# A lightning-attention and mixture-of-depths kernel: from a scheduled order to one pipeline written out by hand over all chunks

## The chip, the cores and the metric

The kernel runs on one core of one Trainium2 chip. The metric is device time in microseconds (us), the median of several executions. The engines are TensorE (PE, with PEld for its weight loads), VectorE (DVE), ScalarE (ACT), GpSimd (POOL) and SyncE (SP, which issues DMAs).

## The reference, cut to what matters

Attention over q, k, v of shape (4 batches, 8 heads, 768 tokens, 64), with a decay `lam` per head, and then a mixture of depths: the 128 tokens of each batch with the highest score go through a two-layer expert, whose result, times a gate, is added to their rows.

```python
# attention, blockwise: scores inside a block, a running state across blocks
intra = (q_b @ k_b.T * lam**(i - j)) @ v_b          # i >= j
inter = (q_b * lam**(i + 1)) @ state
state = lam**block * state + (k_b * lam**(block - 1 - j)).T @ v_b
x = out.transpose(0, 2, 1, 3).reshape(4, 768, 512)  # heads side by side
# mixture of depths, each batch
scores = x @ w_gate
top = 128 tokens with the highest scores
out = x.copy()
out[top] = x[top] + sigmoid(scores[top])[:, None] * (relu(x[top] @ w1) @ w2)
```

All data are fp32; w1 is 512 x 1024 and w2 is 1024 x 512.

## The kernel before, in words

The tokens are cut into chunks of 128, so a batch has six chunks and the whole input 24. `attention_chunk` does one chunk for all eight heads, with two heads (a pair) on the 128 partitions. It loads q, k and v (`qn`, `kn`, `vn`, 256 KB each, SP queue), transposes q and k on PE into `tp` (copied by ACT to `qT`, `kT`), multiplies them to the scores `ss`, masks these on DVE into `p`, and sums `po` from `p` and `vn` and, but for the first chunk of a batch, from `qs` (q times the decay, POOL) and the state. ACT copies `po` to `x_b`, POOL issues its store to `out`, and DVE sums it with `w_gate` to the score column `sc` (tile `xg`). For all but the last chunk of a batch the state is renewed: `kd` (POOL), matmuls `pu`, state times decay (POOL), and the sum of both (DVE).

After the six chunks of a batch come `rank_tokens` and `expert`. The ranks: PE transposes the scores into rows (`pb`, copied to `sc_row`), and DVE counts for each of the six columns of tokens how many scores are larger (`cmp`, L234 to L242). The expert builds two one-hot matrices on DVE: `pick_g` (with the gate `g`, fp32) and `pick`. 24 matmuls `pg` multiply `x_b` by `pick_g`, which gathers the 128 rows, transposed, onto the slots (L271). Six matmuls `pe` give the token of each slot (`tok`). Then come the hidden layer `ph` (w1) with `hs`, the second layer `py` (w2), the copy `y`, and an indirect DMA on POOL that adds `y` to the rows of `out` in HBM (L314).

The kernel is written as plain loops over batches and chunks. The order of the instructions on each engine is set by a planner that goes by dependencies, priorities and free buffers. Both weight matrices are loaded at the beginning, in one DMA of 2 MB each, on ACT's queue, beside the first loads of q, k and v. The buffers: `ld` has 4 of each load, the PSUM pools are two `tp`, two `ss`, one `pu`, one `po` and two shared ones (`pm`) for the expert.

Of the kernel before, what the change touches and what calls it, by code (L numbers as in the profile page):

```python
# [8 lines left out]
FP32 = mybir.dt.float32  # L9
# [8 lines left out]
def kernel(  # L18
# [12 lines left out]
    nc = tc.nc  # L31
# [10 lines left out]
    NGR = (CAP + 127) // 128   # groups of 128 slots  # L42
# [12 lines left out]
    ps_m = ctx.enter_context(tc.tile_pool(name="ps_m", bufs=2, space=PSUM))  # L55

# [22 lines left out]
    # kpow[j, h] = lam_h ** (L - 1 - j)  # L79
# [3 lines left out]
    # with the two heads of a pair on the partitions:  # L83
    # qpow[p, hp, i] = lam ** (i + 1), decay[p, hp, :] = lam ** L
# [13 lines left out]
    # below[i, j] = 1 for j < i  # L98
    below = const.tile([128, 128], FP32, name="below")
    nc.vector.memset(below[:], 1.0)  # L100
    nc.gpsimd.affine_select(
        out=below[:], in_=below[:], compare_op=ALU.is_gt, fill=0.0,
        base=0, pattern=[[-1, 128]], channel_multiplier=1,
    )
    # the slots of each group; in slots_in those past the capacity match no rank
    slots_i = const.tile([128, S], I32, name="slots_i")
    nc.gpsimd.iota(slots_i[:], pattern=[[1, S]], base=0, channel_multiplier=0)
    slots = const.tile([128, S], FP32, name="slots")
    nc.vector.tensor_copy(slots[:], slots_i[:])
    slots_in = const.tile([128, S], FP32, name="slots_in")  # L110
    nc.vector.tensor_copy(slots_in[:], slots_i[:])
    nc.vector.memset(slots_in[:, CAP:], -1.0)
    # the token's place in two columns: start of its chunk, place in the chunk
    place_i = const.tile([128, 1], I32, name="place_i")
    nc.gpsimd.iota(place_i[:], pattern=[[0, 1]], base=0, channel_multiplier=1)
    place = const.tile([128, NT, 2], BF16, name="place")
    for t in range(NT):
        nc.vector.memset(place[:, t, 0:1], float(t * L))
        nc.vector.tensor_copy(place[:, t, 1:2], place_i[:])

# [1 line left out]
    def attention_chunk(b, c, state, x_b, sc):  # L122
        rows = slice(c * L, (c + 1) * L)
        last = c == NT - 1
        qn = ld.tile([128, H, D], FP32, name="qn")
        kn = ld.tile([128, H, D], FP32, name="kn")
        vn = ld.tile([128, H, D], FP32, name="vn")
        for t, src in ((qn, q), (kn, k), (vn, v)):
            nc.sync.dma_start(out=t[:], in_=src[b, :, rows, :].rearrange("h p d -> p h d"))  # L129

        qT = att.tile([128, NHP, L], FP32, name="qT")
        kT = att.tile([128, NHP, L], FP32, name="kT")
        for t, dst in ((qn, qT), (kn, kT)):
            tp = ps_t.tile([128, NHP, L], FP32, name="tp")
            for hp in range(NHP):
                nc.tensor.transpose(  # L136
                    tp[:, hp, :], in_=t[:, 2 * hp : 2 * hp + 2, :], identity=ident[:]
                )
            nc.scalar.copy(out=dst[:], in_=tp[:])  # L139

        if c > 0:
            qs = att.tile([128, NHP, L], FP32, name="qs")
            nc.gpsimd.tensor_tensor(out=qs[:], in0=qT[:], in1=qpow[:], op=ALU.mult)  # L143

        # scores with the keys on the partitions, even and odd heads in two banks
        ss = [ps_s.tile([128, NHP, L], FP32, name="ss") for _ in range(2)]
# [27 lines left out]
        nc.gpsimd.dma_start(out=out[b, rows, :], in_=x_b[:, c, :])  # L174
# [5 lines left out]
        if last:  # L180
            return None

        # state of each pair: the two heads' blocks on the diagonal, zeros beside them
        kd = att.tile([128, H, D], FP32, name="kd")
        nc.gpsimd.tensor_tensor(  # L185
            out=kd[:], in0=kn[:], in1=kpow[:].unsqueeze(2).broadcast_to([128, H, D]),
            op=ALU.mult,
        )
        pu = ps_u.tile([128, NHP, 128], FP32, name="pu")
        for hp in range(NHP):  # L190
            nc.tensor.matmul(  # L191
                pu[:, hp, :],
                lhsT=kd[:, 2 * hp : 2 * hp + 2, :],
                rhs=vn[:, 2 * hp : 2 * hp + 2, :].rearrange("p h e -> p (h e)"),
                start=True, stop=True,
            )
        new = att.tile([128, NHP, 128], FP32, name="state", bufs=3)
        if c == 0:
            nc.gpsimd.memset(new[:], 0.0)
        else:  # L200
            nc.gpsimd.tensor_tensor(out=new[:], in0=state[:], in1=decay[:], op=ALU.mult)  # L201
        for hh in range(2):
            r = slice(hh * 64, (hh + 1) * 64)
            if c == 0:
                nc.vector.tensor_copy(new[r, :, r], pu[r, :, r])
            else:
                nc.vector.tensor_tensor(
                    out=new[r, :, r], in0=pu[r, :, r], in1=new[r, :, r], op=ALU.add
                )
        return new  # L210

# [1 line left out]
    def rank_tokens(sc):  # L213
        sc_row = mod.tile([128, S], FP32, name="sc_row")
        half = (NT + 1) // 2
        for t0 in range(0, NT, half):
            n = min(half, NT - t0)
            pb = ps_m.tile([128, n, 128], FP32, name="pb", tag="pm")
            for t in range(n):
                nc.tensor.transpose(  # L220
                    pb[:, t, :], in_=sc[:, t0 + t : t0 + t + 1].broadcast_to([128, 128]),
                    identity=ident[:],
                )
            nc.scalar.copy(
                out=sc_row[:, t0 * L : (t0 + n) * L], in_=pb[:].rearrange("p t j -> p (t j)")
            )

        parts = mod.tile([128, 3, NT], FP32, name="parts")
        nc.vector.memset(parts[:, 0, 0:1], 0.0)  # L229
        cmp = mod.tile([128, S], FP32, name="cmp")  # L230
        for t in range(NT):
            s = sc[:, t : t + 1]
            if t > 0:
                nc.vector.tensor_scalar(  # L234
                    out=cmp[:, : t * L], in0=sc_row[:, : t * L], scalar1=s, scalar2=None,
                    op0=ALU.is_ge, op1=ALU.add, accum_out=parts[:, 0, t : t + 1],
                )
            nc.vector.tensor_scalar(  # L238
                out=cmp[:, t * L :], in0=sc_row[:, t * L :], scalar1=s, scalar2=None,
                op0=ALU.is_gt, op1=ALU.add, accum_out=parts[:, 1, t : t + 1],  # L240
            )
            nc.vector.scalar_tensor_tensor(  # L242
                out=cmp[:, t * L : (t + 1) * L], in0=sc_row[:, t * L : (t + 1) * L],
# [76 lines left out]
    for b in range(B):  # L320
# [3 lines left out]
        for c in range(NT):  # L324
            state = attention_chunk(b, c, state, x_b, sc)
# [42 lines left out]
```

## Time and profile before

| | |
|---|---|
| median of 3 runs | 316.76 us (316.01 to 317.12) |
| span of the profiled execution | 315.3 us |
| time around that span | not recorded; the median lies 1.5 us above it |
| PE busy | 254.1 us (81%) |
| PE weight loads busy | 220.3 us (70%) |
| DVE, ACT, POOL busy | 124.3, 55.3, 90.3 us |
| HBM read and written | 23.33 and 7.34 MB |

Busy shares are means over stages that have different limits. Matmuls are pipelined and their ends modelled, so a busy PE may still run slowly; the granted clock of PE (1.00 for 2.4 GHz, 0.50 for 1.2 GHz) has to be read beside it.

### The profile page before, as it was taken

The page shows a single profiled execution, that of the slowest core. Times are in us where ns is not written, and L with a number is a line of the kernel's source. Part 1 is how long each engine was busy: PE and PEld are TensorE (multiplying, and loading weights), DVE is VectorE, ACT ScalarE, POOL GpSimd, SP SyncE. Part 2 cuts the span into 40 slices and gives each one's busy share as a digit, 9 for nine tenths or more (in the row PEclk, how much of TensorE's full clock was granted, in tenths as well). Part 3 has the DMA queues.
Part 4 walks back from the last instruction along what each step waited for, and adds up shares of the span by engine and source line. Part 5 has one row for each costly group of instructions (what it writes and reads, how often), then busy time and mean ns, then how long its engine had stood idle before and what let it go on. Part 6 is the DMA issues. An engine that isn't in the chain of part 4 may idle for free.

```text
span 315.3 us, 4666 instructions
## 1 busy us (share of the span) xinstructions
PE 254.1 (81%) x1840; PEld 220.3 (70%) x1840; DVE 124.3 (39%) x385; ACT 55.3 (18%) x101; POOL 90.3 (29%) x97
## 2 busy tenths in 40 slices
PE   1139999956999989955999999965999999609990
PEld 1028989855897789855897789855896789509940
DVE  5312453497120154398120154398120253493000
ACT  2001223420021103320021103330021103200100
POOL 2126537260100358260100358170100355100002
PEclk9999999995589999996589999995599999955997
DMA  6999588790500266591500166590100330100002
GB/s 178 378 267 209 134 202 202 168 227 6 100 2 0 23 180 156 135 224 24 100 2 0 14 187 149 134 187 2 33 0 2 45 123 33 67 0 2 0 0 33
DMA packets 79253, 30.96 MB, mean 98 GB/s; under 512 B 75521, under 2 KB 75521, under 8 KB 79233
## 3 DMA queue, kind: packets, MB, share of 16 engines
q1 hardware_dynamic: 74880, 18.88, 30.0%
q0 software_dynamic: 2496, 7.34, 8.3%
q10 hardware_dynamic: 1856, 4.46, 4.1%
q8 instruction: 14, 0.23, 0.3%
q14 instruction: 7, 0.05, 0.1%
HBM read 23.33 MB, written 7.34 MB: 97 GB/s over the span
## 4 chain that ended last, share of the span: by engine, by line
PE 60%; DVE 19%; issue 7%; SPq 6%; ACT 3%; DMA 2%; POOLq 1%; POOL 0%; DVEq 0%
PE po L169 16%; PE pg L271 12%; PE ph L300 7%; PE py L308 7%; SPq L129 6%; PE po L163 6%; PE ss L150 6%; DVE cmp L238 5%; PE tp L136 4%; DVE p L156 4%; DVE cmp L234 3%; PE pu L191 3%; DVE cmp L242 3%; ACT x_b L173 3%; DVE xg L176 2%
## 5 line engine op out<-in xcount | busy, mean ns | idle before, releaser
L169 PE MATMUL po<-vn,p 128*128 128x64 f32 x384 | 64.5, 287 | 21.4 <-DVE p L156 20.9
L169 PEld LDWEIGHTS po<-vn,p 128*128 128x128 f32 x384 | 57.2, 209 | 26.9 <-DVE p L156 25.0
L176 DVE CUSTOM_DVE_ANT_0 xg<-x_b,wg_b 128x512 f32<-128x512 f32 x24 | 18.5, 772 | 112.5 <-ACT x_b L173 112.5
L271 PE MATMUL pg<-pick_g,x_b 128*128 128x128 f32 x192 | 39.6, 376 | 9.5 <-DVE pick_g L257 9.5
L271 PEld LDWEIGHTS pg<-pick_g,x_b 128*128 128x128 f32 x192 | 35.6, 278 | 11.0 <-issue 11.0
L150 PE MATMUL ss<-qT,kT 64*128 64x128 f32 x384 | 39.0, 307 | 0.0
L191 PE MATMUL pu<-vn,kd 128*128 128x128 f32 x160 | 25.5, 297 | 12.9 <-DMA vn<-in_v_dram 12.3
L163 PE MATMUL po<-state,qs 128*128 128x128 f32 x160 | 35.9, 306 | 0.1
L314 POOL DMA_INDIRECT out_dram<-y,tok x4 | 6.7, 1664 | 98.8 <-ACT y L313 98.8
L201 POOL TENSOR_TENSOR state<-state,decay 128x512 f32<-128x512 f32 x16 | 20.4, 1272 | 49.4 <-DVE parts L229 29.3
L150 PEld LDWEIGHTS ss<-qT,kT 64*128 64x128 f32 x384 | 30.9, 203 | 4.6 <-issue 1.4
L156 DVE TENSOR_TENSOR p<-ss,mask 128x512 f32<-128x512 f32 x48 | 31.0, 683 | 4.6 <-PE ss L150 4.3
L173 ACT COPY x_b<-po 128x512 f32<-128x512 f32 x24 | 14.1, 586 | 106.4 <-PE po L169 106.4
L191 PEld LDWEIGHTS pu<-vn,kd 128*128 128x128 f32 x160 | 22.1, 207 | 13.9 <-issue 8.8
L300 PE MATMUL ph<-gx,w_sb 128*128 128x128 f32 x256 | 29.6, 277 | 0.6 <-ACT gx L276 0.5
L300 PEld LDWEIGHTS ph<-gx,w_sb 128*128 128x128 f32 x256 | 28.9, 192 | 1.3 <-ACT gx L276 1.3
L185 POOL TENSOR_TENSOR kd<-kn,kpow 128x512 f32<-128x512 f32 x20 | 21.3, 1063 | 25.9 <-DMA kn<-in_k_dram 12.3
L308 PE MATMUL py<-w_sb,hs 128*128 128x512 f32 x64 | 28.1, 592 | 0.0
L143 POOL TENSOR_TENSOR qs<-qT,qpow 128x512 f32<-128x512 f32 x20 | 26.0, 1299 | 7.2 <-ACT qT L139 6.9
L163 PEld LDWEIGHTS po<-state,qs 128*128 128x128 f32 x160 | 24.4, 191 | 3.9 <-issue 1.4
L174 POOL DMA_DIRECT2D out_dram<-x_b x24 | 13.9, 580 | 37.8 <-ACT x_b L173 28.0
L136 PE MATMUL tp<-ident,qn 128*128 128x128 f32 x96 | 17.9, 292 | 5.6 <-DMA qn<-in_q_dram 4.7
(57 smaller groups left out, 208.0 us busy)
## 6 DMA issues: line engine op xcount, KB each, us to landing
qn<-in_q_dram SPq DMA_DIRECT2D x24, 256.0 KB, 4.8
kn<-in_k_dram SPq DMA_DIRECT2D x24, 256.0 KB, 5.0
vn<-in_v_dram SPq DMA_DIRECT2D x24, 256.0 KB, 3.3
out_dram<-x_b POOLq DMA_DIRECT2D x24, 256.0 KB, 3.2
w_sb<-in_moe_w_dram ACTq DMA_DIRECT2D x2, 2048.0 KB, 13.7
wg_b<-in_moe_w_gate_dram ACTq DMA_DIRECT2D x1, 256.0 KB, 5.9
out_dram<-y,tok POOLq DMA_INDIRECT x4, 4.9
lam_b<-in_lam_dram ACTq DMA_DIRECT2D x1, 4.0 KB, 3.3
```

The lines of the kernel that those rows point to most:

```text
L136: nc.tensor.transpose(tp[:, hp, :], in_=t[:, 2 * hp : 2 * hp + 2, :], identity=ident[:])
L143: nc.gpsimd.tensor_tensor(out=qs[:], in0=qT[:], in1=qpow[:], op=ALU.mult)
L150: nc.tensor.matmul(ss[hh][:, hp, :], lhsT=kT[r, hp, :], rhs=qT[r, hp, :], start=True, stop=True,)
L156: nc.vector.tensor_tensor(out=p[:, hh::2, :], in0=ss[hh][:], in1=mask[:, hh::2, :], op=ALU.mult)
L163: nc.tensor.matmul(po[:, 2 * hp : 2 * hp + 2, :].rearrange("p h e -> p (h e)"), lhsT=qs[:, hp, :], rhs=state[:, hp, :], start=True, stop=F ...
L169: nc.tensor.matmul(po[:, h, :], lhsT=p[:, h, :], rhs=vn[:, h, :], start=(c == 0), stop=True, skip_group_check=True,)
L173: nc.scalar.copy(out=x_b[:, c, :], in_=po[:].rearrange("p h e -> p (h e)"))
L176: nc.vector.tensor_tensor_reduce(out=xg[:], in0=x_b[:, c, :], in1=wg_b[:], scale=1.0, scalar=0.0, op0=ALU.mult, op1=ALU.add, accum_out=sc[ ...
L191: nc.tensor.matmul(pu[:, hp, :], lhsT=kd[:, 2 * hp : 2 * hp + 2, :], rhs=vn[:, 2 * hp : 2 * hp + 2, :].rearrange("p h e -> p (h e)"), star ...
L271: nc.tensor.matmul(pg[:, dc, :], lhsT=x_b[:, t, dc * 128 : (dc + 1) * 128], rhs=pick_g[:, t, :], start=(t == 0), stop=(t == NT - 1),)
L300: nc.tensor.matmul(ph[:, i, :], lhsT=w1_sb[:, dc, fs], rhs=gx[:, dc, :], start=(dc == 0), stop=(dc == NDC - 1),)
L308: nc.tensor.matmul(py[:], lhsT=hs[:, fc, :], rhs=w2_sb[:, fc, :], start=(fc == 0), stop=(fc == NFC - 1),)
```

## The change

The planner is switched off (`manual_schedule`): every engine runs its instructions in the order in which the program writes them. The chunks of all batches are numbered g = 0 to 23, and `attention_chunk` is cut into four parts, here called by letters: T (`transposes`, with `qs` and `kd`), S (`scores`, with the mask), U (`next_state`) and O (`outputs`, with the store and the score). Step g of the loop issues the loads of chunk g + 4, then T(g + 2), S(g + 1), U(g + 1), O(g), and then the pieces of ranks and expert that a plan has put on this step. For batch b, with s = 6b + 6, the plan puts: the transposes `pb` and the first three counts on step s, three counts on s + 1, the sum of ranks (`total`) on s + 2, `place_of_slots` (picks, `pe`, `tok`) on s + 3, `fetch` on s + 4, `gate` on s + 5, two halves of `hidden` on s + 6 and s + 7, two halves of `back` on s + 8 and s + 9. Pieces of an earlier batch stand ahead of those of a later one in the same step. Steps beyond 23 hold pieces alone.

The rows of the slots are no longer gathered by matmuls with `pick_g`; `fetch` reads them back from `out` in HBM by an indirect DMA (POOL) into `xs`. `gate` transposes `xs` with four transposes and works out the score and gate `g` of the 128 rows. `y` is now `py` times `g` plus `xs` (DVE, one operation), and the indirect DMA writes it over the rows instead of adding. Both indirect DMAs name `out[0 : b + 1]` as their range. The stores of `x_b` move from POOL's queue to SP's. The weights are loaded in eight pieces of 512 KB on SP's queue, two in each of the steps 0 to 3, and `wg_b` behind the loads of chunk 2. Buffers: `ld` 7, `att` 3, and one `tp` for q and one for k, one `ss` for even and one for odd heads. The constants for the ranks are made after T, S and U of the first chunks.

```diff
-    ld = ctx.enter_context(tc.tile_pool(name="ld", bufs=4))
-    att = ctx.enter_context(tc.tile_pool(name="att", bufs=2))
+    ld = ctx.enter_context(tc.tile_pool(name="ld", bufs=AHEAD + 3))
+    att = ctx.enter_context(tc.tile_pool(name="att", bufs=3))
...
-    ps_t = ctx.enter_context(tc.tile_pool(name="ps_t", bufs=2, space=PSUM))
-    ps_s = ctx.enter_context(tc.tile_pool(name="ps_s", bufs=2, space=PSUM))
+    ps_t = ctx.enter_context(tc.tile_pool(name="ps_t", bufs=1, space=PSUM))
+    ps_s = ctx.enter_context(tc.tile_pool(name="ps_s", bufs=1, space=PSUM))
...
+    ctx.enter_context(tc.manual_schedule())
...
-    nc.scalar.dma_start(out=w1_sb[:], in_=moe_w1.rearrange("(c p) f -> p c f", p=128))
-    nc.scalar.dma_start(out=w2_sb[:], in_=moe_w2.rearrange("(c p) e -> p c e", p=128))
+    def load_weights(i):
+        if i < NDC:
+            nc.sync.dma_start(out=w1_sb[:, i, :], in_=moe_w1[i * 128 : (i + 1) * 128, :])
+        else:
+            j = 2 * (i - NDC)
+            nc.sync.dma_start(
+                out=w2_sb[:, j : j + 2, :],
+                in_=moe_w2[j * 128 : (j + 2) * 128, :].rearrange("(c p) e -> p c e", p=128),
+            )
...
-        nc.gpsimd.dma_start(out=out[b, rows, :], in_=x_b[:, c, :])
+        nc.sync.dma_start(out=out[b, rows, :], in_=x_b[:, c, :])
...
+    def rows_upto(b):
+
+        return out[0 : b + 1].flatten_outer_dims()
...
+        def fetch():
+            xs = mod.tile([128, HD], FP32, name="xs")
+            nc.gpsimd.indirect_dma_start(
+                out=xs[:], out_offset=None, in_=rows_upto(b),
+                in_offset=bass.IndirectOffsetOnAxis(ap=keep["tok"][:, :1], axis=0),
+            )
+            keep["xs"] = xs
+
+        def gate():
+            xs = keep["xs"]
+            pt = ps_m.tile([128, NDC, 128], FP32, name="pt", tag="pm")
+            for dc in range(NDC):
+                nc.tensor.transpose(
+                    pt[:, dc, :], in_=xs[:, dc * 128 : (dc + 1) * 128], identity=ident[:]
+                )
+            xsT = mod.tile([128, NDC, 128], FP32, name="xsT")
+            nc.scalar.copy(out=xsT[:], in_=pt[:])
...
+            nc.vector.tensor_tensor_reduce(
+                out=xg[:], in0=xs[:], in1=wg_b[:], scale=1.0, scalar=0.0,
+                op0=ALU.mult, op1=ALU.add, accum_out=g[:],
+            )
...
+        def back(f0):
+            def do():
...
+                for fc in range(f0, f0 + 4):
+                    nc.tensor.matmul(
+                        py[:], lhsT=hs[:, fc, :], rhs=w2_sb[:, fc, :],
+                        start=(fc == 0), stop=(fc == NFC - 1),
+                    )
+                if f0 + 4 < NFC:
+                    return
+                y = mod.tile([128, HD], FP32, name="y")
+                nc.vector.scalar_tensor_tensor(
+                    out=y[:], in0=py[:], scalar=keep["g"][:], in1=keep["xs"][:],
+                    op0=ALU.mult, op1=ALU.add,
+                )
+                nc.gpsimd.indirect_dma_start(
+                    out=rows_upto(b),
+                    out_offset=bass.IndirectOffsetOnAxis(ap=keep["tok"][:, :1], axis=0),
+                    in_=y[:], in_offset=None,
+                )
...
+        s = (b + 1) * NT
+        keep, first, counts = routing(b)
+        for piece in first:
+            put(s, piece)
+        for i, piece in enumerate(counts):
+            put(s + i // 3, piece)
+        s += 2
...
+            put(s + 1, with_rank if i else where)
+            put(s + 2, fetch)
+            for j, piece in enumerate(pieces):
+                put(s + 3 + j, piece)
+
+    transposes(0)
+    load(3)
+    transposes(1)
+    scores(0)
+    next_state(0)
...
+    for g in range(NG):
+        if g + AHEAD < NG:
+            load(g + AHEAD)
+        for i in range(2 * g, min(2 * g + 2, n_w)):
+            load_weights(i)
+        if g + 2 < NG:
+            transposes(g + 2)
+        if g + 1 < NG:
+            scores(g + 1)
+            next_state(g + 1)
+        outputs(g)
+        if g % NT == NT - 1:
+            plan(g // NT)
+        for piece in later.pop(g, []):
+            piece()
+    while later:
+        for piece in later.pop(min(later)):
+            piece()
```

## Rows read from the trace of the kernel before

**Rows 1.** The page: the span.
```profile
span 315.3 us, 4666 instructions
```
**Rows 2.** Busy time by stage: stretch, length, each engine's busy us (instructions), PEclk, DMA.
```profile
61.40:73.90 12.50, 6.33 (x56) 5.29 (x54) 12.36 (x44) 3.34 (x8) 6.49 (x6) 0.92 0.94 168
73.90:91.40 17.50, 17.48 (x86) 15.80 (x86) 5.35 (x22) 1.17 (x2) 1.26 (x1) 0.57 0.23 46
91.40:106.00 14.60, 14.59 (x85) 10.77 (x86) 1.14 (x2) 2.54 (x5) 0.00 (x0) 1.00 0.00 0
106.00:132.50 26.50, 25.39 (x236) 23.54 (x236) 11.08 (x22) 5.86 (x12) 14.38 (x15) 1.00 0.59 140
```
**Rows 3.** Waits of PE: us in total, times, longest us.
```profile
PE po L169 <- DVE p L156: 20.9, 10, 6.1
```
**Rows 4.** Busy time in slices of 1 us, where the granted clock changes.
```profile
71.00:72.00 1.00, 0.00 (x0) 0.00 (x0) 1.00 (x7) 0.00 (x0) 0.00 (x0) 0.89 0.26 39
88.00:89.00 1.00, 1.00 (x7) 1.00 (x6) 0.00 (x0) 0.00 (x0) 0.00 (x0) 0.58 0.00 0
...
276.00:277.00 1.00, 0.00 (x0) 0.00 (x0) 0.96 (x5) 0.00 (x0) 0.00 (x0) 0.79 0.00 0
290.00:291.00 1.00, 1.00 (x10) 1.00 (x10) 0.00 (x0) 0.00 (x0) 0.00 (x0) 0.88 0.00 0
```
**Rows 5.** The chain that ended last, tail: start us, us, what.
```profile
283.96 8.65 PE pg L271 x48
```
**Rows 6.** The chain that ended last, second batch's boundary.
```profile
91.41 7.41 PE ph L300 x64
98.82 6.87 PE py L308 x16
...
120.95 0.89 PE pu L191 x8
121.84 1.15 PE ss L150 x16
...
123.51 0.44 PE tp L136 x4
```
**Rows 7.** Instructions in order of time, one `po`: start us, us, engine, line.
```profile
112.43 0.30 PEld L163 LDWEIGHTS po<-state,qs 128*128 128x128 f32 x2
...
113.10 0.30 PEld L163 LDWEIGHTS po<-state,qs 128*128 128x128 f32 x2
```
**Rows 8.** The page, DMA queues: packets, MB, share of 16 engines' span.
```profile
q1 hardware_dynamic: 74880, 18.88, 30.0%
q0 software_dynamic: 2496, 7.34, 8.3%
q10 hardware_dynamic: 1856, 4.46, 4.1%
```
**Rows 9.** Instructions in order of time, the first transposes of the kernel.
```profile
4.68 1.08 PE L136 MATMUL tp<-ident,qn 128*128 128x128 f32 x4 [4.68 <-DMA qn<-in_q_dram]
```
**Rows 10.** Instructions in order of time, the tail: first and last count, picks, `y`.
```profile
275.04 1.01 DVE L238 TENSOR_SCALAR_CACHE_REDUCE cmp<-sc_row,sc 128x768 f32<-128x768 f32 x1 [0.26 <-ACT sc_row L224]
...
283.26 0.17 DVE L249 TENSOR_TENSOR rank<-rank,parts 128x6 f32<-128x6 f32 x1
...
285.99 0.28 DVE L262 TENSOR_SCALAR pick<-slots,rank 128x128 bf16<-128x128 f32 x1
...
307.60 0.59 ACT L313 COPY y<-py 128x512 f32<-128x512 f32 x1 [6.27 <-PE py L308]
```
**Rows 11.** The page, DMA issues: KB each, median us from issue to landing.
```profile
qn<-in_q_dram SPq DMA_DIRECT2D x24, 256.0 KB, 4.8
...
out_dram<-x_b POOLq DMA_DIRECT2D x24, 256.0 KB, 3.2
w_sb<-in_moe_w_dram ACTq DMA_DIRECT2D x2, 2048.0 KB, 13.7
...
out_dram<-y,tok POOLq DMA_INDIRECT x4, 4.9
```

More of the change, by code (lines that the diff above doesn't have):

```diff
@@ L96, with transposes @@
     nc.vector.tensor_copy(decay[:], qpow[:, :, L - 1 : L].broadcast_to([128, NHP, 128]))
[L99 to L134, printed above, removed]
+    qTs, kTs, qss, kds, ps_, states = {}, {}, {}, {}, {}, {}
+    x_bs, scs = {}, {}
+    def transposes(g):
+        qn, kn, _ = loaded[g]
+        c = g % NT
+        for name, t, keep in (("qT", qn, qTs), ("kT", kn, kTs)):
+            tp = ps_t.tile([128, NHP, L], FP32, name="tp_" + name)
             for hp in range(NHP):
@@ L179, in attention_chunk @@
         )
[L180 to L196, printed above, removed]
@@ L210, in attention_chunk @@
-        return new
-    def rank_tokens(sc):
-        sc_row = mod.tile([128, S], FP32, name="sc_row")
-        half = (NT + 1) // 2
[L216 to L222, printed above, removed]
-                )
[L224 to L243, printed above, removed]
-                scalar=s, in1=below[:], op0=ALU.is_equal, op1=ALU.mult,
-                accum_out=parts[:, 2, t : t + 1],
-            )
-        rank = mod.tile([128, NT], FP32, name="rank")
-        nc.vector.tensor_tensor(out=rank[:], in0=parts[:, 0], in1=parts[:, 1], op=ALU.add)
-        nc.vector.tensor_tensor(out=rank[:], in0=rank[:], in1=parts[:, 2], op=ALU.add)
-        return rank
@@ new lines, in expert, with place_of_slots @@
+    def expert(b, r0, keep):
+        n_in = min(128, CAP - r0)
+        def place_of_slots():
+            rank = keep["rank"]
+            pick = mod.tile([128, NT, 128], BF16, name="pick")
+            for t in range(NT):
+                nc.vector.tensor_scalar(
+                    out=pick[:, t, :], in0=slots[:, r0 : r0 + 128],
+                    scalar1=rank[:, t : t + 1], scalar2=None, op0=ALU.is_equal,
+                )
+            pe = ps_m.tile([128, 2], FP32, name="pe", tag="pm")
@@ L270, in expert @@
             for t in range(NT):
                 nc.tensor.matmul(
-                    pg[:, dc, :], lhsT=x_b[:, t, dc * 128 : (dc + 1) * 128],
-                    rhs=pick_g[:, t, :], start=(t == 0), stop=(t == NT - 1),
-                )
-        gx = mod.tile([128, NDC, 128], FP32, name="gx")
-        nc.scalar.copy(out=gx[:], in_=pg[:])
-        pe = ps_m.tile([128, 2], FP32, name="pe", tag="pm")
-        for t in range(NT):
-            nc.tensor.matmul(
-                pe[:], lhsT=pick[:, t, :], rhs=place[:, t, :],
-                start=(t == 0), stop=(t == NT - 1),
-            )
@@ new lines, in hidden, with do @@
+        def hidden(f0):
+            def do():
+                if f0 == 0:
+                    keep["hs"] = mod.tile([128, NFC, 128], FP32, name="hs")
+                hs, xsT = keep["hs"], keep["xsT"]
+                ph = ps_m.tile([128, 4, 128], FP32, name="ph", tag="pm")
+                for i in range(4):
+                    fs = slice((f0 + i) * 128, (f0 + i + 1) * 128)
+                    for dc in range(NDC):
+                        nc.tensor.matmul(
+                            ph[:, i, :], lhsT=w1_sb[:, dc, fs], rhs=xsT[:, dc, :],
+                            start=(dc == 0), stop=(dc == NDC - 1),
+                        )
+                nc.scalar.activation(hs[:, f0 : f0 + 4, :], ph[:], AF.Relu)
+            return do
@@ new lines, in expert, with put, plan, with_rank @@
+        return (
+            place_of_slots, fetch,
+            [gate] + [hidden(f) for f in range(0, NFC, 4)] + [back(f) for f in range(0, NFC, 4)],
+        )
+    later = {}
+    def put(step, piece):
+        later.setdefault(step, []).append(piece)
+    def plan(b):
+        if NGR == 0:
+            return
+        s = (b + 1) * NT
[5 more added lines that the diff above has]
+        s += 2
+        for i in range(NGR):
+            mine = {} if i else keep
+            mine["rank"] = None
+            where, fetch, pieces = expert(b, i * 128, mine)
+            def with_rank(mine=mine, where=where):
+                mine["rank"] = keep["rank"]
+                where()
+            put(s + 1, with_rank if i else where)
+            put(s + 2, fetch)
+            for j, piece in enumerate(pieces):
+                put(s + 3 + j, piece)
```

242 lines of the change are left out of this document (164 added, 78 removed).

## The prediction

> **What bounds the kernel now.** I read the page first, then the time cut into the stages of one batch, then the waits, then the clock microsecond by microsecond. The span is 315.3 us [rows 1]. One batch repeats every 71 us, and its four stages [rows 2] differ. From 91.4 to 132.5 TensorE (PE) is busy 40.0 of 41.1 us at full clock: matmuls set the time there, while VectorE (DVE) has 1.1 and 11.1 us of work and GpSimd (POOL) 0 and 14.4. From 61.4 to 73.9 PE is busy only 6.3 of 12.5 us and DVE 12.4: DVE counts ranks, and the score masks `p` stand behind the counts on its queue. The wait of `po` for `p` [rows 3] adds up to 20.9 us, 6.1 at the longest. From 73.9 to 91.4 PE is busy all 17.5 us, but at a mean granted clock of 0.57. The reason is in [rows 4]: a slice at 0.89 is at half for its last 0.2 us, so the clock falls at 71.8, some 4 us after the idle of 6.1 began, and comes back only at 88.8: 15 us of dense work ran at 1.2 instead of 2.4 GHz. In the tail it fell at 276.6, and rose at 290.2, 6.3 us after dense work (`pg`) began at 283.96 [rows 5]. So a boundary costs twice: PE idle, then PE at half speed. The gather `pg` by one-hot matmuls is work of its own, 48 records in 8.65 us in the last batch [rows 5].
>
> **Prices of PE work at full clock.** Records are two per fp32 matmul, one per transpose. T (8) 0.88, S (16) 1.15, U (8) 0.89, `ph` 7.41, `py` 6.87 [rows 6]. O: two state and four value records every 0.67 us, four times 2.69 [rows 7]. A full chunk is 5.6 us by this sum. The stage from 106 to 132.5 gives 25.39/236 = 0.108 per record, times 56 records 6.0 [rows 2]; it has small waits that the new order should lose. I take 5.9 us for a step.
>
> **The change, part by part.**
> *Removed:* `pg` (48 records a batch) and the `pick_g` work; in their place four transposes, 0.44 us. At full clock that saves about 5 us a batch, at half clock 10. An expert then costs PE 7.4 + 6.9 + 1.4 for `pb`, `pe` and `gate` = 15.7 us.
>
> *Start.* The weights no longer stand beside the first loads. Engine time per 256 KB [rows 8]: q/k/v 30.0% of 315.3 us over 72 loads = 1.31 us, a store 8.3% over 28 = 0.93, all weights 4.1% = 12.9. The first T began at 4.68 [rows 9], so the keys of chunk 2 land at about 14. T(2), S(1), U(1) and O(0) take 4.7 us at full and 9.5 at half clock: O(0) ends between 18.6 and 23.4, I take 21. Five more steps end at 50.5. Step 6 needs the keys of chunk 8: 25 loads after the first at 1.31, the weights and four stores put them at 4.7 + 32.8 + 12.9 + 3.7 = 54. I take 52 for the start of step 6, bounds 48 (O(0) at its early end) and 56 (transfers 2 us later). In the kernel before, the stage behind batch 0 begins at 61.4 [rows 2].
>
> *Steps 6 to 23.* 16 x 5.9 = 94.4; less what is absent (three chunks without state records, two without U) 4.5; the last two steps 6.5; two whole experts 31.4; the small pieces of batch 2, 1.0. Together 128.8. DVE and POOL have room: 11.1 and 14.4 us stood beside 25.4 of PE [rows 2], and the counts, 8.4 us from 275.04 to 283.43 [rows 10], are split over two steps behind that step's `p`, so `p` waits for at most half of them and is needed a step later. I cost that at nothing where the earlier expert's `hidden` covers it, at 0.7 us for batch 0, where nothing does.
> Waits that are new: `place_of_slots` puts six picks on DVE and at once six `pe` matmuls on PE. For batches 1 and 2 the picks stand behind `y` of the batch before, which needs that batch's last `py`. PE stands for y 0.7 (the copy in its place took 0.59) + picks 1.3 (half of the twelve that ran from 283.43 to 286.27 [rows 10]) + 0.2 = 2.2 us, with the next step's T, S, U and O queued behind it; for batch 0, 2.7. Sum 7.1. `fetch` has a step, about 6 us, to land before `gate`. The trace shows no gather: the nearest row is the indirect scatter, 4.9 us from issue to landing, the ends are a store's 3.2 and the weights' 13.7 [rows 11]. I take 4.9, so it is hidden; at 8 it would cost 2 us a batch. Stores move from POOL to SP, behind the loads of the step, and hold back the loads of the next one until O is copied; those have two steps (12 us) to land against a median of 4.8 [rows 11]: nothing. POOL loses 24 issues. PE end of O(23): 52 + 128.8 + 7.1 + 0.7 = 188.6.
>
> *Tail,* from O(23)'s end. `fetch` of batch 2 must wait for the landing of batch 1's scatter, since its source holds those rows, and the last two steps are short: `gate` starts 2.0 late. Transposes and copy to 3.1, `hidden` 3.7 to 6.8, and only then, PE being in order, `pb` and its copies to 8.5. Counts run to 16.9, but PE's other half of `hidden` and `back` of batch 2 run to 18.6, and `y` and then the picks stand behind that. Tokens are known at 21.4 (`y` 0.7, picks 1.3, `pe` and three small DVE operations 0.8, an estimate). The scatter of batch 2, issued at 19.4, lands at 24.3; the fetch of batch 3 waits for it and lands at 29.2. PE has been idle for 8 us then, so it is at half clock: transposes 1.1 [rows 9] and copy 0.65 to 30.9, `hidden` and `back` 14.3, plus 2.4 until the clock rises 6.3 us after the restart, to 47.6. From the start of `y` to the end 7.7 [rows 10]. Tail 55.4; before, the first count began 40.3 us before the end [rows 1, 10], without another batch's 14.3 us of matmuls behind it.
>
> Against the row of 4.9 us stands the Trainium skill, "DMA: Bandwidth & Descriptors", section "Anatomy of one DMA": a GpSimd DMA takes about 2.0 us plus bytes over 436 GB/s, 2.6 us for 256 KB (an estimate from that page). By it the two landings in the tail would give back 4.6 us, and the time be about 241. The scatter measured here adds into HBM and the new one does not, so the row may be too high; the sum keeps it.
>
> **Sum.** 188.6 + 55.4 = 244.0 us of span. No time but the span is known of the profiled execution; the median of the runs, 316.76, lies 1.5 us above it. So 245.5 us. A difference below 0.3% (1 us) could not be told from none.
>
> **The rivals.**
> 1. *As summed, 236 to 254 us.* Chance 0.58.
> 2. *Shorter, below 236.* A gather and a plain scatter that land like a store (3.2) take 3.4 off the tail's two waits, step 6 at 48 takes 4, a chunk of 5.6 us 5: 233. For it speaks that the sum of [rows 6, 7] is 5.6; against it that the densest stage did not reach that. Chance 0.11. What the Trainium skill's fit above gives back would fall to this case.
> 3. *The clock falls inside the loop.* The waits of 2.2 to 2.7 us at `place_of_slots` are shorter than the idle of 4 us after which it fell [rows 4], but the trace shows none of this length. Each fall would cost 3 to 7 us (half of 6.3 to 14.6 us at half clock): three give 255 to 267. Chance 0.12.
> 4. *The start is bound by transfers.* If the eight 512 KB pieces of the weights did not overlap, each would take at least the 3.2 us of a store's landing [rows 11]: 25.6 instead of 12.9, and step 6 would begin 13 us later: 258. Against it, loads with a landing of 4.8 us cost the engines 1.31 each, so they run over each other. Chance 0.12. The Trainium skill, "DMA: Bandwidth & Descriptors", section "Rules for kernel authors", speaks for this one: at least 1 MiB a transfer for full bandwidth, where the kernel before moved 2 MB at once. By that rule 258 would be the time; the trace before has no piece of 512 KB.
> 5. *The change does not do what it says:* `p` again ends up behind the counts, three boundaries idle 6.1 us and lose 7 at half clock, 39 more: 285. The order of DVE speaks against it. Chance 0.03.
> 6. *Slower.* The clock does not rise at all. At 73.9 a dense mix of `ss`, `po` and `pg` kept PE busy for 15 us without raising it [rows 2, 4], and the new loop is a mix everywhere. The 70 us gained are gone once about 66 us of the 190 us of full-clock work run at half. Against it, the steady mix from 106 to 132.5 held 1.00. Over 320 us; chance 0.04.
>
> **Range and chances.** Cases 1 to 4 lie between 233 and 267. The range 231 to 264 leaves out cases 5 and 6 (0.07), part of 3 and of 2, some 0.15 in all. Faster 0.95, same 0.01, slower 0.04.
>
> **What would show it.** In the changed profile: O of chunk 5 at 48 to 56 us; granted clock 1.00 from about 20 us to the last chunk, with three short PE gaps at `pe`; no wait of `po` for `p` above 1 us; no `pg` group; last chunk's O at about 189; a gap of PE of some 8 us behind the last `place_of_slots`, ended by the fetch, and the fetch held by a scatter; half clock at its end. The prediction is wrong if the clock falls between 25 and 185 us, if T waits for loads after step 8, or if POOL, with scatter, fetch and the state in one queue, makes U or O wait.

## The result

The changed kernel takes 249.72 us (median of 4 runs, 248.14 to 253.99), the kernel before, beside it on the same chip, 316.38 (4 runs): a ratio of 0.789 [0.783, 0.795]. Forecast were 245.5 us, 231 to 264. The profiled execution took 248.36 us, its span is 246.7 against a forecast sum of 244.0. The ratios leave out executions more than 1.5% above the fastest of their kernel (one of these four, and some of e2 to e4 and e9 to e12 below), the medians don't.

### The profile page after: what moved, and what is told of

Its sections match the earlier page's. It is cut to its first block, busy times and chain, and to the rows that moved or that the text cites. A ratio compares the mean times of both kernels' runs of the same rounds, so it can differ in the third digit from the quotient of the medians.

```text
span 246.7 us, 4281 instructions
## 1 busy us (share of the span) xinstructions
PE 213.3 (86%) x1664; PEld 182.8 (74%) x1664; DVE 130.2 (53%) x371; ACT 51.3 (21%) x97; POOL 79.4 (32%) x77
## 4 chain that ended last, share of the span: by engine, by line
PE 53%; SPq 13%; DVE 11%; issue 10%; DMA 8%; ACT 2%; POOLq 1%
PE po L217 10%; SPq L68 10%; PE ph L360 9%; PE py L373 8%; PE ss L158 8%; DMA kn<-in_k_dram 7%; PE po L211 6%; PE pu L177 5%; PE tp_kT L133 3%; PE tp_qT L133 2%; DVE pick L299 2%; DVE p L164 2%; DVE cmp L269 2%; SPq L84 1%; DMA xs<-out_dram,tok 1%
## 5 line engine op out<-in xcount | busy, mean ns | idle before, releaser
L217 PE MATMUL po<-vn,p 128*128 128x64 f32 x384 | 53.5, 268 | 0.0
L217 PEld LDWEIGHTS po<-vn,p 128*128 128x128 f32 x384 | 51.4, 198 | 0.0
L158 PE MATMUL ss<-qT,kT 64*128 64x128 f32 x384 | 32.9, 314 | 2.4 <-DVE p L164 2.2
L360 PE MATMUL ph<-xsT,w_sb 128*128 128x128 f32 x256 | 32.8, 291 | 1.4 <-ACT xsT L335 1.4
L360 PEld LDWEIGHTS ph<-xsT,w_sb 128*128 128x128 f32 x256 | 31.7, 206 | 2.1 <-ACT xsT L335 2.0
L158 PEld LDWEIGHTS ss<-qT,kT 64*128 64x128 f32 x384 | 27.4, 212 | 7.3 <-issue 3.8
L224 DVE CUSTOM_DVE_ANT_0 xg<-x_b,wg_b 128x512 f32<-128x512 f32 x24 | 17.1, 711 | 26.9 <-ACT x_b L221 26.6
L145 POOL TENSOR_TENSOR kd<-kn,kpow 128x512 f32<-128x512 f32 x20 | 21.4, 1071 | 8.6 <-DVE kpow L106 5.4
L133 PE MATMUL tp_qT<-ident,qn 128*128 128x128 f32 x96 | 16.1, 294 | 7.7 <-DMA qn<-in_q_dram 7.7
L187 POOL TENSOR_TENSOR state<-state,decay 128x512 f32<-128x512 f32 x16 | 21.3, 1330 | 1.1 <-DVE state L193 1.1
L269 DVE TENSOR_SCALAR_CACHE_REDUCE cmp<-sc_row,sc 128x768 f32<-128x768 f32 (+5 forms) x24 | 16.2, 675 | 9.7 <-ACT sc_row L250 9.7
L373 PEld LDWEIGHTS py<-w_sb,hs 128*128 128x128 f32 x64 | 11.7, 190 | 12.4 <-issue 12.4
L137 ACT COPY qT<-tp_qT 128x512 f32<-128x512 f32 x24 | 14.1, 586 | 28.4 <-PE tp_qT L133 28.3
```

What stands on the lines that cost most here:

```text
L133: nc.tensor.transpose(tp[:, hp, :], in_=t[:, 2 * hp : 2 * hp + 2, :], identity=ident[:])
L145: nc.gpsimd.tensor_tensor(out=kd[:], in0=kn[:], in1=kpow[:].unsqueeze(2).broadcast_to([128, H, D]), op=ALU.mult,)
L158: nc.tensor.matmul(ss[hh][:, hp, :], lhsT=kT[r, hp, :], rhs=qT[r, hp, :], start=True, stop=True,)
L187: nc.gpsimd.tensor_tensor(out=new[:], in0=states[g][:], in1=decay[:], op=ALU.mult)
L217: nc.tensor.matmul(po[:, h, :], lhsT=p[:, h, :], rhs=vn[:, h, :], start=(c == 0), stop=True, skip_group_check=True,)
L360: nc.tensor.matmul(ph[:, i, :], lhsT=w1_sb[:, dc, fs], rhs=xsT[:, dc, :], start=(dc == 0), stop=(dc == NDC - 1),)
```

## The profile after

The page of the changed kernel first: span, busy time, the clock in 40 slices, DMA queues.
```profile
span 246.7 us, 4281 instructions
PE 213.3 (86%) x1664; PEld 182.8 (74%) x1664; DVE 130.2 (53%) x371; ACT 51.3 (21%) x97; POOL 79.4 (32%) x77
PEclk9999999799999799999998599999998899985897
q1 hardware_dynamic: 80144, 29.63, 53.1%
q0 software_dynamic: 640, 2.10, 2.7%
```
PE is busy for 86% of the span. The clock falls four times in the loop, for 3.4 to 6.8 us each, and once in the tail, instead of for some 17 us behind a batch [rows 4]. Its waits (us in total, times, longest):
```profile
PE tp_qT L133 <- DMA qn<-in_q_dram: 7.7, 4, 5.1
PE pe L305 <- DVE pick L299: 6.6, 6, 1.8
PE pt L331 <- DMA xs<-out_dram,tok: 5.7, 1, 5.7
PE ss L158 <- DVE p L164: 2.2, 2, 1.4
```
Of the first, 5.1 us are the first loads of the kernel. The wait of `po` for `p` [rows 3], 20.9 us, is gone; 2.2 us of `ss` for `p` are left. New are `pe` for the picks, and one wait for the fetch. Busy time by stretch, for [rows 2] (length, busy us of PE, PEld, DVE, ACT, POOL, clock, DMA): steps 7 to 9, the place of batch 0, a plain step, the places of batches 1 and 2, the tail.
```profile
57.70:79.00 21.30, 18.81 (x174) 17.28 (x172) 20.47 (x56) 5.51 (x12) 11.61 (x9) 1.00 0.89 188
79.00:88.40 9.40, 7.59 (x56) 6.79 (x57) 4.36 (x15) 1.63 (x3) 1.15 (x1) 0.82 0.63 142
88.40:94.10 5.70, 5.70 (x58) 5.41 (x57) 2.83 (x6) 1.58 (x4) 2.73 (x3) 1.00 0.83 182
...
133.50:143.10 9.60, 8.05 (x53) 7.33 (x53) 3.52 (x7) 1.17 (x2) 2.44 (x3) 0.64 0.25 68
...
186.50:194.40 7.90, 6.58 (x47) 5.78 (x46) 3.85 (x12) 0.00 (x0) 2.01 (x2) 0.78 0.22 66
198.00:246.70 48.70, 34.70 (x181) 24.91 (x178) 15.11 (x58) 5.20 (x11) 2.95 (x3) 0.86 0.06 22
```
A plain step is 5.7 us, PE busy without a gap. Steps 7 to 9, from 57.7 to 79.0, take 21.3 us instead of three times 5.7; there it is DVE that is full (20.47 of 21.30). The three places have gaps and a reduced clock, here in slices of 1 us (same columns) where it falls and rises:
```profile
83.00:84.00 1.00, 1.00 (x14) 1.00 (x14) 0.00 (x0) 0.59 (x2) 0.90 (x1) 0.60 1.30 254
86.00:87.00 1.00, 1.00 (x7) 1.00 (x8) 0.00 (x0) 0.00 (x0) 0.00 (x0) 0.69 0.10 29
134.00:135.00 1.00, 0.00 (x0) 0.00 (x0) 1.00 (x2) 0.00 (x0) 0.97 (x1) 0.70 0.71 240
141.00:142.00 1.00, 1.00 (x10) 1.00 (x10) 0.00 (x0) 0.00 (x0) 0.00 (x0) 0.88 0.00 0
189.00:190.00 1.00, 1.00 (x12) 1.00 (x12) 0.39 (x3) 0.00 (x0) 0.00 (x0) 0.51 0.68 262
192.00:193.00 1.00, 1.00 (x8) 1.00 (x9) 0.04 (x1) 0.00 (x0) 0.11 (x1) 0.78 0.39 61
```
A slice at 0.60 is at half speed for its last 0.8 us. So half speed lasts from 83.2 to 86.6, 134.4 to 141.2 and 189.0 to 192.4: 13.6 us in three falls. DMA issues (KB each, median us to landing) for [rows 11]:
```profile
out_dram<-x_b SPq DMA_DIRECT2D x24, 256.0 KB, 2.2
w_sb<-in_moe_w_dram SPq DMA_DIRECT2D x8, 512.0 KB, 5.9
...
xs<-out_dram,tok POOLq DMA_INDIRECT x4, 3.4
out_dram<-y,tok POOLq DMA_INDIRECT x4, 2.8
```
And the tail, in order of time (start, us, engine), for [rows 10]:
```profile
215.84 0.99 POOL L384 DMA_INDIRECT out_dram<-y,tok  x1 [23.73 <-DVE pick L299]
217.52 0.15 DVE L317 CAST tok<-tok_f 128x1 int32<-128x1 f32 x1
219.34 0.97 POOL L321 DMA_INDIRECT xs<-out_dram,tok  x1 [2.51 <-issue]
222.81 1.12 PE L331 MATMUL pt<-ident,xs 128*128 128x128 f32 x4 [5.72 <-DMA xs<-out_dram,tok]
224.60 9.96 PE L360 MATMUL ph<-xsT,w_sb 128*128 128x128 f32 x64 [0.67 <-ACT xsT L335]
241.47 0.75 DVE L380 SCALAR_TENSOR_TENSOR y<-py,g,xs 128x512 f32<-128x512 f32 x1 [16.43 <-PE py L373]
```
The tokens of batch 3 are known at 217.67. Its fetch is issued 1.67 us later: the scatter of batch 2, issued at 215.84, must land first. The row gives no releaser (`issue`); in e10 the trace names that landing for the same kind of wait (3.3 us). `ph` takes 9.96 us instead of 7.41 [rows 6], since the clock comes back only at about 230.

## The experiments

Steps are read off the starts of the copies `x_b` (start of step g+1 = end of O(g)), in each run's profiled execution; the tail runs from O(23) to the end of the span. "O(6..9) one by one" gives the steps that end with O(6) to O(9), and 9>10 the time from O(9) to O(10). Those that carry the reading, in us:

```
              O(0)   O(5)   O(9)   O(23)  tail | O(6..9) one by one | 9>10  15>16 21>22
after         19.85  52.61  78.97  198.05 48.7 | 5.1 6.3 7.2 7.7    | 9.43  14.80 11.36
e1            19.93  52.64  78.91  183.71 53.5 | 5.0 6.3 7.2 7.8    | 5.36   8.47  7.53
e3            19.00  47.25  73.28  193.97 51.2 | 4.8 6.3 7.2 7.7    | 7.84  13.70 13.17
e8            19.16  47.41  73.45  178.25 41.3 | 4.8 6.3 7.2 7.8    | 5.36   8.47  7.53
e9            19.36  51.25  76.58  195.96 47.4 | 5.6 6.3 5.9 7.4    | 11.95 12.31  9.77
e10           18.80  47.08  71.34  182.79 42.3 | 4.8 6.3 5.7 7.4    | 5.62   8.46  7.53
```

**e1, picks early.** The six picks of `place_of_slots` become a function of their own, put behind the rank additions; `pe` stays a step later.
```
...
-            put(s + 1, with_rank if i else where)
+            put(s, picks)
+            put(s + 1, where)
...
```


> Picks a step earlier, pe where it was. If the three waits of PE for the picks (2.8, 3.6 and 2.3 us in the changed kernel) also bring the clock down (half from 83.2, 134.4 and 189.0 us, for 3 to 7 us each), both go: 7 us of waits and some 6 us of half clock, about 236 us, and the clock stays at 1.00 from 50 to 218 us. If instead DVE is the limit there, the picks only move the wait to the next mask p, the clock still falls, and the time stays above 246 us.

239.65 us (238.44 to 241.39), ratio 0.756 [0.749, 0.763]. The clock in 40 slices of its page, and its tail by the columns above:
```profile
PEclk9999999889999999999999999999999679965999
183.70:237.20 53.50, 37.11 (x180) 27.24 (x180) 14.99 (x58) 5.20 (x11) 2.95 (x3) 0.84 0.06 20
```
No wait of `pe` for picks and no fall at the three places: 4.07 + 6.33 + 3.83 = 14.2 us shorter there, of which 6.6 were waits, and 7.6 the clock (half of 13.6 is 6.8). But the tail is 4.8 longer: the last steps being short now, `gate` of batch 2 waits 1.6 us for a fetch that the scatter of batch 1 holds, and the clock is at half from 185.7 to 192.5.

**e2, batch 3 first.** After the last chunk batch 3's rank, places and fetch go ahead of the rest of batch 2's `back`.
```
...
-    while later:
-        for piece in later.pop(min(later)):
-            piece()
+    rest = [piece for s in sorted(later) for piece in later[s]]
+    for piece in last["head"] + rest[:3] + last["where"] + rest[3:] + last["pieces"]:
+        piece()
```


> Behind the last chunk, ranks, picks, pe and fetch of batch 3 stand ahead of what remains of batch 2. If the tail is set by PE's in-order queue and by the fetch that waits for batch 2's scatter, batch 2's matmuls cover the counts and the fetch's landing, PE does not go idle at 217 and keeps 2.4 GHz: 9 to 10 us less, about 240 us. If the counts (8.4 us on DVE) and the fetch are a chain that the matmuls cannot cover, at most 3 us less: 247 us or more.

240.89 us (239.07 to 243.09), ratio 0.756 [0.748, 0.765]. O(23) at 199.47, and then, by the columns above:
```profile
199.00:238.70 39.70, 31.68 (x185) 22.29 (x183) 15.00 (x58) 5.11 (x11) 2.95 (x3) 0.99 0.08 27
```
The tail is 39.2 instead of 48.7 us, at full clock. The falls inside the loop remain.

**e3, weights spread.** One piece of the weights in each of steps 2 to 9, instead of two in steps 0 to 3.
```
-        for i in range(2 * g, min(2 * g + 2, n_w)):
-            load_weights(i)
+        if 2 <= g < 2 + n_w:
+            load_weights(g - 2)
```


> One piece of the weights in each of the steps 2 to 9 instead of two in the steps 0 to 3. If the weights in front of the loads make T wait (7.7 us for q, 1.0 for k) and let the clock fall at 45.7, O of chunk 5 ends at about 47 instead of 52.6 and the time is about 244 us. If DVE's backlog in batch 0's counts (steps 7 to 9 of 6.3, 7.2 and 7.7 us) sets the time there, or the transfers are short of the same bytes a little later, the gain is lost by step 10: 248 us or more.

245.92 us (243.28 to 250.16), ratio 0.769 [0.761, 0.776]. O(5) comes 5.4 us earlier and O(9) still 5.7; the falls at 45.7 and at 83 are absent. The clock in 40 slices of its page, and its waits for the picks:
```profile
PEclk9999999999999999999997999999975569975899
PE pe L305 <- DVE pick L299: 6.6, 6, 1.8
```
PE waits for the picks as long as in the changed kernel (1.79 us at the first place), and yet the clock stays at 1.00 there: that place takes 7.84 us, 2.5 more than in e1, where the changed kernel with its fall loses 4.1. The lead is 7.3 us at O(10), but only 1.5 at the end of this execution (245.2 against 246.7): behind the last place half speed lasts from 180.4 to 200.9, where the changed kernel had 3.4 us of it.

**e6, weights first.** Both weights in two transfers of 2 MB on ScalarE's queue ahead of the first loads.
```
+    nc.scalar.dma_start(out=w1_sb[:], in_=moe_w1.rearrange("(c p) f -> p c f", p=128))
+    nc.scalar.dma_start(out=w2_sb[:], in_=moe_w2.rearrange("(c p) e -> p c e", p=128))
...
-        for i in range(2 * g, min(2 * g + 2, n_w)):
-            load_weights(i)
```


> All weights at the very start, two DMAs of 2 MB on ACT's queue, as in the kernel before. If late loading is worth the time that 4.2 MB take (12.9 us of all engines), the first chunks start 8 to 12 us later: 258 to 262 us. If the first 50 us are bound by the same bytes in either order, it makes no difference: 248 to 252 us.

257.33 us (256.8 to 257.92), ratio 0.811 [0.804, 0.817]. The second T waits 11.7 us for its queries:
```profile
PE tp_qT L135 <- DMA qn<-in_q_dram: 16.7, 2, 11.7
```
O(0) ends at 32.62, 12.8 later, O(5) at 60.92, 8.3 later. Late weights are worth 8 us of the 67 gained.

**e4, no hand-written order.** `tc.manual_schedule()` is dropped; **e12** does the same to e8 below.
```
-    ctx.enter_context(tc.manual_schedule())
```


> The changed kernel without the order written by hand: the planner orders the instructions again, everything else (rows fetched and written by indirect DMA, late weights, pieces given in the new sequence) stays. If the hand-written order carries the gain, the ranks and the expert run mostly between batches again and the time is 265 us or more. Rival: the new operations and the sequence in which the program gives them carry it, and the planner keeps them between the chunks: 255 us or less.

> e8 without the order written by hand, the planner orders again. e4 had 245.6 and 253.1 us where the hand-ordered kernel has 248 to 254, so the hand order is worth nothing there. If it is worth nothing in general (the sequence in which the program gives the pieces is what counts), 219 to 223 us. Rival: the planner hides in e4 the picks' waits that e8 takes out by hand and has waits of its own instead (matmuls of po for p 5.4 us, of pt for the fetch 11.8 us in three places): 228 us or more.

e4: 245.61 and 253.08 us, against 248.14 to 253.99 with the hand order: no difference that two runs can show. e12: 237.2 us (232.29 to 237.8), ratio 0.738 [0.732, 0.744], against e8's 0.697 [0.693, 0.700]. So the order itself brought no visible part of this change's gain; once the picks, the weights and the tail are mended by hand, it is worth 12 to 13 us (by the lowest times, 220.1 and 232.3, and by the ratios). In e12 `pu` waits for GpSimd's `kd` (3.7 us) and `po` for `p` (3.9) again.

**e5, no spreading.** All pieces of a batch in one step of the next.
```
-            put(s + i // 3, piece)
-        s += 2
+            put(s, piece)
...
-                put(s + 3 + j, piece)
+                put(s, piece)
```


> The changed kernel with all pieces of a batch put on one step of the next batch, so that ranks, places, fetch and expert run in one stretch. The last tail of the changed kernel takes 48.7 us, of which about 5 are the landing of the last rows and about 16 the expert's matmuls that the loop pays anyway; if overlap carries the gain, each of the three boundaries is longer by 15 to 27 us: 295 to 330 us. Rival: TensorE's sum of work is the bound and the waits are filled by the next chunk's transposes and scores: 265 us or less.

296.39 us (295.41, 297.37), ratio 0.934 [0.926, 0.942]. One boundary, and its largest wait:
```profile
57.10:97.50 40.40, 24.39 (x155) 19.12 (x153) 14.96 (x57) 4.32 (x9) 5.65 (x5) 0.79 0.27 59
PE pe L305 <- DVE pick L299: 42.9, 4, 10.8
```
PE idles 16 of 40.4 us at each of three boundaries and runs at half clock behind it: put on one step, the pieces cost 47 of the 67 us.

**e7, gather by matmuls.** `pg` and its weighted picks come back into the new order, and the scatter adds.
```
-        pt[:, dc, :], in_=xs[:, dc * 128 : (dc + 1) * 128], identity=ident[:]
+        pg[:, dc, :], lhsT=x_bs[b][:, t, dc * 128 : (dc + 1) * 128],
+        rhs=keep["pick_g"][:, t, :], start=(t == 0), stop=(t == NT - 1),
...
+                nc.scalar.copy(out=y[:], in_=py[:])
...
-                    in_=y[:], in_offset=None,
+                    in_=y[:], in_offset=None, compute_op=ALU.add,
```


> The changed kernel with the expert's input gathered again by 24 matmuls against one-hot columns (pg, 8.65 us for 48 in the kernel before's tail), the gate's factor carried in the picks, and y added to the rows by the scatter. If the fetch by indirect DMA pays by what it takes from TensorE and VectorE: about 5 us more in each of three batches in the loop, and in the tail 4.3 us of pg and a scatter that lands in 4.9 instead of 2.8 us, against 6 us of waiting for the fetch (2.5 + 3.4) that goes: about 265 us. Rival: pg fills the gaps in which the clock falls (four falls of 3 to 7 us at half speed in the loop and 10 us in the tail), and the fetch's waits go: 252 us or less.

260.6 us (258.76 to 260.81), ratio 0.819 [0.814, 0.825]. `pg` and the scatter:
```profile
L334 PE MATMUL pg<-pick_g,x_b 128*128 128x128 f32 x192 | 24.0, 289 | 0.3 <-DVE ext L321 0.3
out_dram<-y,tok POOLq DMA_INDIRECT x4, 5.2
```
The rival was half right: the clock does not fall at the places of batches 1 and 2 (1.00 from 137 to 149 and from 190 to 206 us), which are 5.6 and 3.1 us shorter. But it isn't `pg` that fills the gaps, as it comes two steps later (from 153.54): `pe` hardly waits there (0.3 us), since `y` is now a copy on ACT and the picks no longer stand behind it on DVE. At the first place the wait and a fall are still there. And `pg` costs more than the two places give: a step with it takes 10.2 us instead of 5.2, O(23) comes at 204.80, 6.8 later (2.1 of which were there at O(6), before any piece that e7 changes), and the tail is 5.6 longer. The scatter that adds lands in 5.2 us, the plain one in 2.8.

**e9, without `qs` and `kd`.** Leaves out GpSimd's two scalings of a chunk; unscaled queries and keys are used.
```
-            nc.gpsimd.tensor_tensor(out=qs[:], in0=qTs[g][:], in1=qpow[:], op=ALU.mult)
+            qss[g] = qTs[g]
...
-            kds[g] = kd
+            kds[g] = kn
```


> Leaves out GpSimd's two multiplications of a chunk: the queries scaled by powers of the decay (qs) and the keys scaled (kd); the unscaled ones are used, so the output is another. Theory: VectorE's operations with two inputs in SBUF stand still beside these two: the rank additions and the counts' equality (573 ns mean) and picks (354 ns) fall to their short values (about 0.17, 0.36 and 0.28 us), and steps 7 to 9 (6.3, 7.2 and 7.7 us) go towards 5.7: 3 to 6 us off the loop, about 244 us. Rival: the long operations have another cause and VectorE's backlog is just its sum of counts: those means stay and the time stays within 1 us of 249.7, less what the first score of each chunk no longer waits.

245.02 us (241.99 to 246.53), ratio 0.767 [0.759, 0.775]. The occasion was this stretch of the changed kernel, GpSimd's rows and then DVE's:
```profile
74.92 1.71 POOL L187 TENSOR_TENSOR state<-state,decay 128x512 f32<-128x512 f32 x1 [1.12 <-DVE state L193]
76.59 1.04 POOL L145 TENSOR_TENSOR kd<-kn,kpow 128x512 f32<-128x512 f32 x1
75.42 1.22 DVE L283 TENSOR_TENSOR rank<-parts 128x6 f32<-128x6 f32 x1
76.68 0.97 DVE L284 TENSOR_TENSOR rank<-rank,parts 128x6 f32<-128x6 f32 x1
```
Additions of six numbers, 0.16 us in the tail, take 1.22 and 0.97, and end at 76.64 and 77.65, when GpSimd's operations end (76.63, 77.63). Means of the three groups (busy us, mean ns) in the changed kernel and then in e9:
```profile
L273 DVE SCALAR_TENSOR_TENSOR cmp<-sc_row,sc,below 128x128 f32<-128x128 f32 x24 | 13.8, 573 | 0.9
L283 DVE TENSOR_TENSOR rank<-parts 128x6 f32<-128x6 f32 x4 | 1.7, 425 | 0.0
L284 DVE TENSOR_TENSOR rank<-rank,parts 128x6 f32<-128x6 f32 x4 | 1.5, 367 | 0.1
```
```profile
L266 DVE SCALAR_TENSOR_TENSOR cmp<-sc_row,sc,below 128x128 f32<-128x128 f32 x24 | 8.4, 352 | 0.9
L276 DVE TENSOR_TENSOR rank<-parts 128x6 f32<-128x6 f32 x4 | 1.7, 423 | 0.0
L277 DVE TENSOR_TENSOR rank<-rank,parts 128x6 f32<-128x6 f32 x4 | 0.7, 166 | 0.1
```
What stood beside `qs` or `kd` is short now; the first addition, beside GpSimd's state multiplication, which stays, is as long as before (1.22 us in both). So DVE stands still there for GpSimd, as the Trainium skill has it ("SBUF — State Buffer", section "SBUF: two separate sides"): the two share a pair of ports, and an operation of DVE with two inputs in SBUF waits out the whole GpSimd instruction that came first; the ends above agree with it to 0.02 us. It explains 1.5 us of steps 7 to 9 (19.7 instead of 21.2); what is left of the 4.2 above three steps of 5.7 I put down to the sum of the counts, which no run leaves out.

**e8, all three** (e1, e2 and e3 together), **e10** (batch 0's counts two a step, its expert a step later, `gate` of batch 2 behind the last chunk) and **e11** (e8 with the counts two a step, the ranks' sum and places a step later, fetch and expert where they were). e10 against e8:
```
-                put(s + i // 3, piece)
-        s += 2
+                put(s + i // (2 if b == 0 else 3), piece)
+        s += 3 if b == 0 else 2
...
-                put(s + 3 + j, piece)
+                put(s + (4 if b == B - 2 else 3) + j, piece)
...
```


> The picks a step ahead of the place matmuls, the weights one piece a step, and batch 3's ranks, places and fetch ahead of the rest of batch 2's expert, together. If the three act in different stretches, the sum is that of e1's end of the loop (183.7) less 5.5 (the start, as O(9) came 5.7 earlier in e3) plus e2's tail of 39.2, and 1.6 more for the gate of batch 2 waiting for its fetch at step 23 as in e1: 179 + 39.2 + 1.6 = 219 us of span, 221 us. Rival: they share one cause, the clock (a fall avoided at one place comes at another): 232 us or more.

> As e8, with batch 0's counts two a step in place of three (and its expert one step later), and batch 2's gate after the last chunk, behind batch 3's score rows. If steps 7 to 9 are long because VectorE can't do three counts beside the chunk's own work in one step, about 3 of their 4 us above three steps of 5.7 go, and the gate's wait of 1.6 us at step 23 goes: 216 to 218 us. Rival: those steps are held by something else (GpSimd's state multiplications, or transfers) and the gate's wait only moves: within 1.5 us of e8.

> As e8, with batch 0's counts two a step, its rank additions, picks and place matmuls one step later, and its fetch and expert on their old steps (in e10 the expert one step later met batch 1's fetch). If what e10 won in steps 6 to 9 (25.1 against 26.6 us) stays and its loss was the later expert alone: 219 to 220 us. Rival: the fetch issued in the same step as the places lands too late for the gate of step 11 (about 4.5 us after its issue, in a step of 5.7), TensorE waits and the clock falls: 222 us or more.

e8: 220.87 us (220.11 to 222.19), ratio 0.697 [0.693, 0.700]; O(23) at 178.25, tail 41.3 us, as added up. Its clock:
```profile
PEclk9999999999999999999999999999999997999998
```
e10: 227.87 us (225.18 to 229.74), ratio 0.711 [0.706, 0.717]. Steps 7 to 9 are 1.8 us shorter, but batch 0's scatter now comes a step later, batch 1's fetch waits 3.3 us for its landing, `gate` for the fetch 3.7 (longest), and the clock falls there. e11: 221.8 us (219.67 to 224.38), ratio 0.696 [0.692, 0.700], which is e8's: what the counts gain, the later places of batch 0 give back (O(9) 73.32 against 73.45, O(12) 91.10 against 89.73). The 25.1 and 26.6 us that were expected from are the times from O(6) to O(10) in e10 and e8.

## Why the forecast held, step by step

**The pieces between the chunks** carry most of the gain, as forecast: with all of them on one step (e5) 47 of 67 us are gone. The gather adds 11 (e7), late weights 8 (e6). Each was taken out of the changed kernel by itself, so the three need not add up. The stores on SP's queue, the buffers, the split PSUM pools and the late constants were not varied, and what they are worth is not shown.

**Start.** O(0) 19.85 (21), O(5) 52.61 (52). The sizes held, the reason only in part. Transfers did delay it, but one step ahead of the keys that I had named: T(7) waits for its queries and keys, 1.05 and 0.57 us, the clock falls at 45.7, and that step takes 9.2 us. With the weights spread (e3) neither the waits nor the fall is there. The fourth rival's 13 us did not come. The rule of the Trainium skill cited there ("DMA: Bandwidth & Descriptors", "Rules for kernel authors") did not decide: pieces of 512 KB landed in 5.9 us, and two of 2 MB, sent first, cost 8 us.

**A step.** 5.7 us, not 5.9: 16 of them gave 3.2 us back. The sum of records from [rows 6, 7] was the better price than the mean of a stage with small waits.

**`place_of_slots`.** Its waits were 6.6 us (7.1). The step that failed is that they cost nothing more, "shorter than the idle of 4 us after which it fell": the third rival's mechanism came, three falls, and the places cost 14.2 us in all (e1). It cost 2.5 us a fall, under that rival's 3 to 7, as the clock rose after 3.4, 6.8 and 3.4 us. That is this execution: behind like waits half speed lasted from nothing to 20.5 us in e3.

**Counts of batch 0.** Put at 0.7 us, they cost 4.2 in steps 7 to 9, for DVE is full there: three counts a step beside `p`, state and `xg`, and operations that GpSimd holds (e9). "DVE and POOL have room" was read off a stretch in which no counts ran.

**O(23)** thus came at 198.05, not 188.6: +0.6 from the start, +7.1 from the places, +3.5 from the counts, -3.2 from the steps; 1.4 us are not assigned.

**Tail.** 48.7 us, not 55.4. The tokens came 19.6 us after O(23), where 21.4 less the 2.0 of a late gate is 19.4. The gate was not late (-2.0), since the falls had made the last steps long; in e1, without them, it was, and the tail 53.5. From the scatter's issue to the fetch's landing it took 7.0 us, not 9.8, and from `y` to the end 5.2, not 7.7. The row of 4.9 us [rows 11] was for a scatter that adds, which e7 confirms (5.2); the plain one lands in 2.8, the fetch in 3.4. The estimate of 2.6 us by the Trainium skill, "DMA: Bandwidth & Descriptors", "Anatomy of one DMA", is close to the plain scatter's 2.8 and under the fetch's 3.4. `ph` at half clock, +2.5, was right (2.4).

So the forecast time was met because two errors of opposite sign, +9.4 and -6.7 us, nearly cancel. That the number was so close is luck; that the boundaries lost their idle time and most of their half speed is not. The condition that I had set for being wrong (the clock falls between 25 and 185 us) did occur.

**Open:** what decides whether a short gap lets the clock fall, and for how long. Behind the same wait at the first place (1.78 to 1.79 us) it did not fall in e3, and was at half for 3.4 us in the changed kernel and for 6.8 in e2 and in e6. In e9 the wait was 1.61 us and half speed lasted from 78.8 to 92.4 with PE busy, so that the first place and the step behind it took 19.5 us there, in the changed kernel 15.1:
```profile
PEclk9999999799999559999999799999999999965999
```
e1 and e7 show that no fall came at the places where the wait was gone. A difference of 2 or 3 us between two single traces may be no more than this.

## What to carry to other kernels

Where one engine's short results (here six picks) are asked for in the same piece by TensorE, put a whole step between them: in the profiled execution the wait itself was half the cost, the clock behind it the other half. When a serial tail is left, hand the last batch's chain of dependent steps to the engines first and keep independent matmuls back to cover it; it saved 9.5 us of the tail here and added up with the rest (e8: 220.9 us). A shorter step elsewhere can make a hidden transfer late (e1's gate, e10's fetch): look at what stands next before counting a gain.

## What was not expected of the hardware

The clock fell where TensorE was never idle for long. Around 133 us the gaps were 1.04 and 1.54 us, beside six small `pe` matmuls, and half speed lasted 6.8 us. Before 45.7 they were 1.05 and 0.57 us, at 80.72 there was one of 1.79. At 83.2 and 189.0 it fell in a slice in which PE was busy throughout, 1.4 and 0.2 us after dense work had begun again. How long half speed then lasted, with PE busy for most of it, went from 3.4 us to 13.7 (e9) and 20.5 (e3). In the kernel before it fell in idle of 6.1 us [rows 3, 4].

What GpSimd holds on VectorE is not only long operations: an addition of six numbers took 1.22 us instead of 0.16, and a pick 1.80 instead of 0.28 (in e9, without `kd`, the longest took 0.46).

An indirect scatter of 128 rows that adds lands in 4.9 to 5.2 us, one that only writes in 2.8; an indirect fetch of as many takes 3.4 in the changed kernel (medians of 3.4 to 4.8 in the others).
